# One attention and gated-MLP kernel: score operands moved 64 bytes, score products of 64 rows, down and output columns cut 256 and 320

## The chip, the cores and the metric

The kernel runs on one core of one Trainium2 chip. Five engines take part: TensorE (PE, matrix products; PEld is its loading of the stationary operand), VectorE (DVE), ScalarE (ACT), GpSimd (POOL), and SyncE (SP), whose queue issues most of the DMAs. The metric is the device time of one execution in microseconds (us); lower is better. Three executions of the kernel before took 2593.94, 2594.28 and 2596.97 us, so its median is 2594.28 us.

## What is computed

An attention block and a gated MLP read the same normalised input, and the MLP's result, through silu, gates the attention's:

```python
x = A_x                                      # 1 x 2048 x 576
xn = _layernorm(x, axis=-1)
s = _A_ref(xn, A_wqkv, A_wo)                 # 32 heads of 18: softmax(q k^T / sqrt(18)) v, then @ wo
g = _silu(_B_ref(xn, B_w_gate, B_w_up, B_w_down))   # ((xn @ w_gate) * (xn @ w_up)) @ w_down, 4608 wide
return x + s * g
```

Everything is float32. The kernel splits a float32 operand into a high part, which TensorE's float32r format holds, and a low part, the rest, and adds up high x high, high x low and low x high.

## The kernel before, in words

**Stages.** First the input is normalised, turned into columns (`xc`), and multiplied with `wqkv`: `qk_block` (L493) makes q and k, block by block of 128 columns, from a weight tile that is the stationary operand (`wgu`, `wq1` or `wq2`) and `xc` as the moving one; each block is 14 products of 128 rows by 512 columns, 13 with the weight tile and one with `ninth`. `v_block` (L556) makes v. Results go to DRAM. Then comes the long main stage, from about 193 to 2525 us, in which attention and MLP run side by side. Last, `L1469` multiplies the attention's columns with `wo` and the rows are finished.

**The main stage.** TensorE's array is used as two halves of 64 rows: rows 0 to 63 and rows 64 to 127, each with its own stream of products. Their kinds are:

- up and gate (`gu_op`, L813), 27 products of 512 columns to a group, up in half 0 and gate in half 1, with weights `wgu` stationary and `xc` moving;
- down (`down_op`, L874), `hs` stationary and `wd` moving. The 576 columns of the result go in two parts of `HALF` = 288, so a part is one product of 288 columns, 6 to a group in each half;
- score products for the row maxima (`a_item`, L709), one product of 512 columns each, 64 to a head, reduced by VectorE (L711). They stand in half 0, but for the first head, whose products go to both;
- score products for the exponentials (`b_item`, L761), 64 to a head as well, followed by ScalarE's exponential (L763). They stand in half 1, but for the end of the last head;
- value products (`pv_group`, L772), which use all 128 rows, so both halves stop for them.

**The score operands.** For each head a stack holds three times 18 rows of q or of k (high and low parts), `R` = 54 rows in each half of a tile. `turning` has one side and `whole0`/`whole1`, alternating by head, the other: `stacks_of` says which is which. L761 reads two rows more, 56: they carry minus the row maximum, high and low, against ones on the other side. L638 and L641 fill the three tiles with 1.0 on POOL, and `load_stack` (L322) brings the rows in by DMA on SP's queue.

**Where tiles lie.** The pools on the right-hand side of SBUF end at its top, so what a pool holds in all decides where it begins. In the program before, `turning`, `whole0` and `whole1` (pool `stk`) begin at bytes 204768, 212960 and 221152 of each partition, all 224 past a multiple of 256. `wq2`, in the pool `early` in the same place before it, lies 224 past a multiple of 256 as well. `xc`, `wgu`, `wq1`, `ninth`, `hs`, `wd` and `wos` all lie 160 past one. A column slice of 288 floats is 1152 bytes, so the second part of `wd` and of `wos` begins 32 past a multiple of 256. Every other slice that the products of 512 columns take begins a multiple of 512 bytes into its tile and keeps the tile's offset.

**The order.** The program is issued in an order that Python works out while it builds the kernel (`order`, L1326 on). Each half has a clock, `clk[0]` and `clk[1]`; the half whose clock is behind gets the next product: a score product if its bank is free and its due time has come, else down or up and gate. After a product the half's clock goes on by a planned duration: 0.231 us for 512 columns, 0.132 us for a part of down. `engine` keeps account of VectorE, ScalarE and POOL in the same way (0.685 us for a reduction, 0.596 for an exponential, 0.41 or 0.45 for the drain of a part of down). TensorE runs its instructions in the order of issue; nothing is decided on the chip.

**Drains.** A finished part of down is added to `acc` by VectorE (L937), or copied to `st` by ScalarE (L931) and added by POOL (L901).

Of the kernel before, what the change touches and what calls it, by code (L numbers as in the profile page):

```python
# [20 lines left out]
FT = mybir.dt.float32  # L21
FR = mybir.dt.float32r
I32 = mybir.dt.int32
AF = mybir.ActivationFunctionType
OP = mybir.AluOpType
# [16 lines left out]
def kernel(  # L42
# [10 lines left out]
    nc = tc.nc  # L53
    _, S, D = x.shape
    F = w_gate.shape[1]
    H = 32
    DH = D // H
    assert S == 2048 and D == 576 and F % 256 == 0
    NT = S // 128
    NCH = S // 512  # L60
    NF2 = F // 256
    HALF = D // 2
    scale = float(DH) ** -0.5
    PSUM = bass.MemoryType.PSUM

# [541 lines left out]
    for c in range(NCH):  # L607
        if c + 2 < NCH:
            load_x(c + 2)
        for b in range(3):  # L610
            qk_block(b, c)
            if c == 0 and b == 0:
                w_now(2)
        if c + 1 < NCH:
            to_columns(c + 1)
        for b in range(3, 6):
            qk_block(b, c)
            if c == 1 and b == 3:
                v_split(c)
            if b < 5 and c + 2 < NCH:  # L620
                norm(c + 2, (0, 1) if b == 3 else (2, 3))
            if c in (1, 2):
                x_store(c, range(3 * (b - 3), 3 * (b - 2)))
            if c == 0 and b == 3:
                v_fetch(1)
            if c == NCH - 1 and b == 3:
                w_now(3)
        if c == 1:
            w_fetch(3)
            for t in range(4):  # L630
                v_block(t)
            w_fetch(4)
        if c == 2:
            w_now(4)
    early.close()
    stk = ctx.enter_context(tc.tile_pool(name="stk", bufs=1, side="right", reuse_waits="tile"))
    turning = stk.tile([128, S], FR, name="turning")
    nc.gpsimd.memset(turning.bitcast(FT), 1.0)  # L638
    whole = [stk.tile([128, S], FR, name=f"whole{i}") for i in range(2)]
    for w in whole:  # L640
        nc.gpsimd.memset(w.bitcast(FT), 1.0)  # L641
    vmore = ExitStack()
    more_rows(vmore.enter_context(tc.tile_pool(name="vmore", bufs=1, side="right")), 2)
    g_load(0)
# [46 lines left out]
    with ExitStack() as mid:  # L691
# [3 lines left out]
        def load_v(g):  # L695
            vt[g] = mp.tile([128, NT, 2 * (DH + 1)], FT, name="vt", bufs=2)
            nc.sync.dma_start(vt[g].rearrange("p t (h d) -> p t h d", h=2), sv[:, 2 * g:2 * g + 2, :].rearrange("(t p) h d -> p t h d", p=128))

        mx = {}

        def a_item(h, i, r=0, tag="a"):

            t, c = divmod(i, 4)
            if i == 0:
                mx[h] = mp.tile([128, NT, 4], FT, name="mx", bufs=1)
            q, k = stacks_of(h, r)
            p = bank(tag, 2)
            rows = slice(64 * r, 64 * r + R)
            nc.tensor.matmul(p, q[rows, t * 128:(t + 1) * 128], k[rows, c * 512:(c + 1) * 512],  # L709
                             start=True, stop=True)  # L710
            nc.vector.tensor_reduce(mx[h][:, t, c:c + 1], p, axis=AX.X, op=OP.max)  # L711
# [42 lines left out]
        def b_item(h, i, r=1, tag="b"):  # L754
            t, c = divmod(i, 4)
            if c % 2 == 0:
                pt[t, c // 2] = mp.tile([128, 2, 512], FT, name="pt", bufs=PT)
            q, k = stacks_of(h, r)
            p = bank(tag, 2)
            rows = slice(64 * r, 64 * r + R + 2)  # L760
            nc.tensor.matmul(p, k[rows, t * 128:(t + 1) * 128], q[rows, c * 512:(c + 1) * 512],  # L761
                             start=True, stop=True)
            nc.scalar.activation(pt[t, c // 2][:, c % 2, :], p, AF.Exp, scale=scale)  # L763
# [37 lines left out]

        hs, us = {}, {}
        TERMS = [t for b in range(9) for t in ((b, b, 0), (9 + b, b, 0), (b, b, 1))]
        half = [slice(0, 64), slice(64, 128)]

        def gu_start(r, n):
            ready(gdone, n)
# [63 lines left out]
        def down_op(r, u, s, i, ps, n, by):  # L871
            own = alone(u, 2 * s + i)
            j, a, e = DTERMS[n]
            op = nc.tensor.matmul(ps[:, 0:HALF], hs[u][half[r], j, a, s * 128:(s + 1) * 128],  # L874
                             dw[u][half[r], j, e, i * HALF:(i + 1) * HALF],
                             start=(own or r == 0) and n == 0, stop=(own or r == 1) and n == len(DTERMS) - 1)
            if not own and r == 0 and n == len(DTERMS) - 1:
                handing[u, s, i] = by.nop()
                after(handing[u, s, i], op)
            if not own and r == 1 and n == 0:  # L880
                after(op, handing.pop((u, s, i)))
# [33 lines left out]

        def down_end(u, s, i, ps, act):
            c, q = units[u]
            cs = slice(i * HALF, (i + 1) * HALF)
            if q == 0 and c >= 2:
                ready(sdone, 4 * c - 8 + s)  # L920
            a = sums(4 * c + s)[:, cs]
            if s == 3:
                seen[u] = seen.get(u, 0) + 1
                if seen[u] == 2:
                    d_get(u + 1)
            if act:
                if q == 0:
                    nc.scalar.activation(a, ps[:, 0:HALF], AF.Copy)
                else:
                    st = mp.tile([128, HALF], FT, name="st", bufs=2)  # L930
                    nc.scalar.activation(st, ps[:, 0:HALF], AF.Copy)  # L931
                    sums_later.append((a, st, u, s))
                    return
            elif q == 0:
                nc.vector.tensor_copy(a, ps[:, 0:HALF])
            else:
                nc.vector.tensor_tensor(a, a, ps[:, 0:HALF], op=OP.add)  # L937
            down_summed(u, s)

        def down_summed(u, s):  # L940
# [80 lines left out]
            nc.sync.dma_start(wos[1].bitcast(FT), swo[:, 8:10, :])  # L1021

        passed, xdone, xhalf = {}, [], set()

        def stream(r, kind):

            def glu(n):
                c, q = units[n // 2]
                box = []
                for k in range(len(TERMS)):  # L1030
                    def work(k=k):
                        if k == 0:
                            box.append(gu_start(r, n))
                        gu_op(r, n, box[0], k)
                        if q == NF2 - 1 and n % 2 and k % 3 == 2 and c < NCH - 1:
                            b = k // 3
                            if (c, b) in xhalf:
                                x_block(c + 1, b)
                                there["x", c + 1, b] = moved(clk[r] + 0.5, 0.40)
                            xhalf.add((c, b))  # L1040
                        if n == 2 * len(units) - 1 and k == 13:
                            xdone.append(r)
                            if len(xdone) == 2:
                                wo_fetch()
                        if k == len(TERMS) - 1:
                            highs.append((gate_end if r else up_end)(n, box[0]))
                    end = (("DVE", 0.685) if r else ("ACT", 0.595)) if k == len(TERMS) - 1 else None
                    yield 0.231, k == 0, work, end, ("g", n, k), len(TERMS)

            def down(u, n):  # L1050
                own = alone(u, n)
# [2 lines left out]
                for k in range(len(DTERMS)):  # L1054
# [7 lines left out]
                    end = None  # L1062
                    if (own or r) and k == len(DTERMS) - 1:
                        end = (None, 0.0)
                    yield 0.132, (own or r == 0) and k == 0, work, end, ("d", u, 6 * n + k), len(DTERMS)

            if kind == "g":
                for n in range(2 * len(units)):
# [29 lines left out]
        due, jobs, rows_done = [], [], {}  # L1098
        there, queue = {}, [0.0]
        na = nb = 0  # L1100
        part_work = len(units) * (2 * 27 * 0.231 + 4 * 12 * 0.132)
        part = part_work + (TOTAL + N + LEAD) * 0.231
        span = part + H * NT * (0.858 + 0.06)
        QUICK, LAST = 0.65, 0.6
        pace = (PACE * span - QUICK * N - LAST * (N + LEAD)) / (TOTAL - N)
# [3 lines left out]
        def keep_course(now):  # L1109

            left = part_work - (gone[0] + gone[1]) / 2
            left += (2 * TOTAL - na - nb) * 0.1155 + (H * NT - nb // 4 + len(due)) * 0.918
            course[:] = [na, now, (EASE * left - TAIL - LAST * (N + LEAD)) / (TOTAL - na)]

        def a_goal(i):
# [24 lines left out]
        def a_next(r=0):  # L1140
# [5 lines left out]
            slot = turn[tag] % 2  # L1146
            turn[tag] += 1
            banks[tag][slot] = engine("DVE", clk[r] + 0.43, 0.685) + SPARE
            clk[r] += 0.231
            na += 1  # L1150
            if na % 32 == 0 and N <= na < TOTAL - N:
                keep_course(clk[r])
# [8 lines left out]
        def b_next(r=1):  # L1161
# [8 lines left out]
            turn[tag] += 1  # L1170
            end = engine("ACT", clk[r] + 0.43, 0.596)
            banks[tag][slot] = end + SPARE
            clk[r] += 0.231
            nb += 1
            if i % 4 == 3:
                due.append((h, i // 4, end + 0.1))
# [149 lines left out]
        def order():  # L1326
# [5 lines left out]
            while going(0) or going(1) or na < TOTAL or nb < TOTAL or due or jobs or soon or pool_later:  # L1332
# [33 lines left out]
                elif op is not None:  # L1366
# [14 lines left out]
                        kept[n, k // 6] = slots[0, kind]  # L1381
                    if end:
                        if kind == "d":
                            end = ("ACT", 0.41) if acts[-1] else ("DVE", 0.45)
                        if kind == "g" and r == 0 and n in by_dve:
                            end = ("DVE", 0.685)
                        done = engine(end[0], clk[r] + 0.20, end[1])
# [27 lines left out]
    with ExitStack() as end:  # L1415
# [45 lines left out]
        for i, t in enumerate(order):  # L1461
# [4 lines left out]
            for h in range(2):  # L1466
                for n, (a, e) in enumerate(PAIRS):
                    w = wos[0][:, a, :] if a < 8 else wos[1][:, a - 8, :]
                    nc.tensor.matmul(ps[h][:, 0:HALF], oc[:, e, :], w[:, h * HALF:(h + 1) * HALF],  # L1469
                                     start=n == 0, stop=n == len(PAIRS) - 1)  # L1470
            if i + 5 < NT:
                fetch_o(order[i + 5])
# [5 lines left out]
            g = gin.pop(t) if t < 12 else last_gates[t - 12]  # L1478
            xt = xi.pop(t)
            for h in range(2):  # L1480
                cs = slice(h * HALF, (h + 1) * HALF)
                nc.vector.tensor_tensor(y[:, cs], ps[h][:, 0:HALF], g[:, cs], op=OP.mult)
                if t == order[-1]:
                    nc.vector.tensor_tensor(y[:, cs], y[:, cs], xt[:, cs], op=OP.add)
                    nc.sync.dma_start(out2[t * 128:(t + 1) * 128, cs], y[:, cs])
# [34 lines left out]
```

## Time and profile before

| | |
|---|---|
| median of three runs | 2594.28 us |
| span of the profiled execution | 2590.2 us |
| TensorE, share of the span | 100% |
| VectorE, ScalarE, POOL | 70%, 60%, 26% |
| DMA, mean rate | 168 GB/s |
| first product of the main stage | 193.5 us |
| last down product begins | 2525.4 us |

The page gives for each engine its busy time and count of instructions; then the span in slices; then the chain of work that ended last, followed back from the end; then groups of instructions by line with the mean duration of one and the idle time before them. A product's recorded duration is modelled and overlaps the next one's, so the distance from start to start is what tells how fast TensorE goes. In the chain of waits and the timeline, each row has a start, a length, and how many instructions it merges (x94). `64*128 64x512` is a product of 64 rows by 128 stationary columns, with 512 moving columns.

### The profile page before, as it was taken

Reading aid. Unit: us, or ns where it says so; the run is one execution under the profiler, and the core shown is the slowest. Engines: PE = TensorE matmul, PEld = TensorE weight load, DVE = VectorE, ACT = ScalarE, POOL = GpSimd, SP = SyncE. Lnnn points to the kernel's source line nnn. Section 1 sums busy time; section 2 is a strip of 40 time slices with the busy share of each in tenths; the row PEclk is TensorE's granted clock in tenths of the full one; section 3 lists DMA queues with packets and bytes.
Section 4 is the critical chain, followed back from the end, with each engine's and each line's share of the span. In section 5 each row is a group of like instructions: output and inputs, shape, how many; then the busy total and the mean of one; then the engine's idle time right before and its main releaser. Section 6 shows DMA issues by size and latency. Waiting matters only on the chain.

```text
span 2590.2 us, 59629 instructions
## 1 busy us (share of the span) xinstructions
PE 2582.3 (100%) x24439; PEld 2124.4 (82%) x24439; DVE 1815.2 (70%) x2996; ACT 1551.5 (60%) x3092; POOL 677.0 (26%) x701
## 2 busy tenths in 40 slices
PE   9999999999999999999999999999999999999999
PEld 8899877888888888888877877778888877877889
DVE  7209777776777778777777877777777777777238
ACT  4224677766766666666666666666666666666621
POOL 3114444434431222222111222111111222221016
PEclk9999999999999999999999999999999999999999
DMA  7899767677653444444454443444444444443357
GB/s 237 258 301 260 200 184 196 184 189 214 178 189 111 141 164 136 150 162 160 143 166 148 142 142 126 137 146 159 121 158 124 145 150 142 133 139 112 125 202 253
DMA packets 186641, 435.65 MB, mean 168 GB/s; under 512 B 51104, under 2 KB 112192, under 8 KB 156160
## 3 DMA queue, kind: packets, MB, share of 16 engines
q1 hardware_dynamic: 184208, 423.88, 53.0%
q0 software_dynamic: 2160, 7.96, 0.8%
q8 instruction: 192, 3.15, 0.5%
q14 instruction: 81, 0.66, 0.1%
HBM read 315.16 MB, written 111.35 MB: 165 GB/s over the span
## 4 chain that ended last, share of the span: by engine, by line
PE 98%; DMA 1%; DVE 1%; SPq 0%; ACT 0%; issue 0%; DVEq 0%
PE pg L813 36%; PE pg L772 17%; PE pg L874 16%; PE pa L709 11%; PE pb L761 9%; PE pb L493 2%; PE pa L493 2%; PE pg L556 2%; PE pg L1469 1%; PE pb L1469 1%; PE pa L1469 1%; DMA oin<-sot 0%; PE pa L761 0%; DMA xin<-in_A_x_dram 0%; PE pg L402 0%; DVE mx L711 0%
## 5 line engine op out<-in xcount | busy, mean ns | idle before, releaser
L711 DVE TENSOR_REDUCE mx<-pa 128x1 f32<-128x512 f32 x2016 | 1349.2, 687 | 330.5 <-PE pa L709 151.5
L813 PE MATMUL pg<-xc,wgu 64*128 64x512 f32 x7776 | 1441.6, 391 | 0.0
L763 ACT ACTIVATE pt<-pb 128x512 f32<-128x512 f32 x2005 | 1145.0, 602 | 469.0 <-PE pb L761 347.3
L813 PEld LDWEIGHTS pg<-xc,wgu 64*128 64x128 f32 x7776 | 1074.9, 186 | 51.9 <-issue 1.0
L874 PE MATMUL pg<-wd,hs 64*128 64x288 f32 x6816 | 879.0, 293 | 0.0
L874 PEld LDWEIGHTS pg<-wd,hs 64*128 64x128 f32 x6816 | 816.3, 185 | 11.3 <-issue 0.8
L709 PE MATMUL pa<-whole,turning 54*128 54x512 f32 x1999 | 783.2, 399 | 0.3 <-DVE mx L711 0.3
L761 PE MATMUL pb<-whole,turning 56*128 56x512 f32 x1978 | 775.2, 398 | 0.0
L772 PE MATMUL pg<-pt,vt 128*32 128x512 f32 x4096 | 453.3, 594 | 0.1
L709 PEld LDWEIGHTS pa<-whole,turning 54*128 54x128 f32 x1999 | 363.3, 184 | 76.6 <-issue 53.0
L854 POOL TENSOR_TENSOR hs<-us,hs 128x512 fp32r<-128x512 f32 x144 | 186.1, 1292 | 865.8 <-ACT hs L838 612.4
L901 POOL TENSOR_TENSOR acc<-acc,st 128x288 f32<-128x288 f32 x284 | 229.5, 810 | 606.3 <-ACT st L931 314.4
L761 PEld LDWEIGHTS pb<-whole,turning 56*128 56x128 f32 x1978 | 360.1, 185 | 5.8
L772 PEld LDWEIGHTS pg<-pt,vt 128*32 128x32 f32 x4096 | 126.2, 110 | 285.1 <-issue 279.2
L778 DVE TENSOR_TENSOR oc<-oc,pg 128x512 f32<-128x512 f32 x35 | 24.1, 688 | 221.1 <-PE pg L772 207.0
L257 POOL TENSOR_TENSOR wgu<-wraw,wgu 128x384 fp32r<-128x384 f32 x108 | 108.2, 1015 | 212.8 <-ACT wgu L256 118.1
L776 ACT ACTIVATE oc<-pg 128x512 f32<-128x512 f32 x32 | 19.2, 599 | 229.4 <-PE pg L772 222.0
L937 DVE TENSOR_TENSOR acc<-acc,pg 128x288 f32<-128x288 f32 x261 | 116.3, 448 | 38.2 <-PE pg L874 35.4
L830 DVE TENSOR_TENSOR us<-pg,us 128x512 f32<-128x512 f32 x144 | 98.7, 685 | 54.9 <-PE pg L813 52.2
L931 ACT ACTIVATE st<-pg 128x288 f32<-128x288 f32 x284 | 117.1, 413 | 27.2 <-PE pg L874 20.0
L823 ACT ACTIVATE us<-pg 128x512 f32<-128x512 f32 x143 | 85.5, 598 | 76.2 <-PE pg L813 63.8
L838 ACT ACTIVATE hs<-us 128x512 fp32r<-128x512 f32 x142 | 89.4, 630 | 16.2 <-DVE us L830 15.8
(164 smaller groups left out, 1294.5 us busy)
## 6 DMA issues: line engine op xcount, KB each, us to landing
wgu<-swg SPq DMA_DIRECT2D x102, 1152.0 KB
wd<-swd SPq DMA_DIRECT2D x50, 1152.0 KB
swg<-wgu SPq DMA_DIRECT2D x36, 1152.0 KB
whole<-sqk SPq DMA_DIRECT2D x192, 144.0 KB
turning<-sqk SPq DMA_DIRECT2D x384, 72.0 KB
swd<-wd SPq DMA_DIRECT2D x18, 1152.0 KB
sqk<-hl SPq DMA_DIRECT2D x32, 512.0 KB
xc<-sx SPq DMA_DIRECT2D x24, 512.0 KB
```

The source lines that it names most:

```text
L257: nc.gpsimd.tensor_tensor(w[:, 9 + b:12 + b, :], raw[:, b:b + 3, :], w[:, b:b + 3, :].bitcast(FT), op=OP.subtract)
L709: nc.tensor.matmul(p, q[rows, t * 128:(t + 1) * 128], k[rows, c * 512:(c + 1) * 512], start=True, stop=True)
L711: nc.vector.tensor_reduce(mx[h][:, t, c:c + 1], p, axis=AX.X, op=OP.max)
L761: nc.tensor.matmul(p, k[rows, t * 128:(t + 1) * 128], q[rows, c * 512:(c + 1) * 512], start=True, stop=True)
L763: nc.scalar.activation(pt[t, c // 2][:, c % 2, :], p, AF.Exp, scale=scale)
L772: nc.tensor.matmul(p[32 * c:32 * c + 32, :], vt[h // 2][:, t, 6 * (h % 2):6 * (h % 2) + 32], pt[t, c // 2][:, c % 2, :], start=t == ts[0], ...
L813: nc.tensor.matmul(ps, gw[n][half[r], a, :], xg[i][half[r], e, :], start=k == 0, stop=k == len(TERMS) - 1)
L854: nc.gpsimd.tensor_tensor(hj[:, 1, :], h32, hj[:, 0, :].bitcast(FT), op=OP.subtract)
L874: op = nc.tensor.matmul(ps[:, 0:HALF], hs[u][half[r], j, a, s * 128:(s + 1) * 128], dw[u][half[r], j, e, i * HALF:(i + 1) * HALF], start=( ...
L901: nc.gpsimd.tensor_tensor(a, a, st, op=OP.add)
L931: nc.scalar.activation(st, ps[:, 0:HALF], AF.Copy)
L937: nc.vector.tensor_tensor(a, a, ps[:, 0:HALF], op=OP.add)
```

## The change

Four things are changed together.

1. A tile of 64 bytes, `gap`, is added to the pools `early` and `stk`. Both pools grow by 64 bytes at a fixed upper end, so `wq2` and the three score tiles begin 64 bytes lower: `turning` at 204704, which is 160 past a multiple of 256.
2. L709 and L761 read all 64 rows of a half instead of 54 and 56. So that the added rows add nothing, they are filled with 0 on one side and 1 on the other: rows 32 to 63 and 96 to 127 of each tile get a memset of their own, six in place of three; the loads bring in the rows below 54 as before.
3. The 576 columns of down and of the output product are cut 256 and 320 instead of 288 and 288, and so are the drains of those parts. The second part begins 1024 bytes into its row.
4. The planned durations in the order are changed: 512 columns 0.2267 us, parts of down 0.120 and 0.1467 us, and the drains of a part by its size.

```diff
+    PARTS = (slice(0, 256), slice(256, D))
+    WIDTH = (256, D - 256)
...
             if c == 0 and b == 0:
                 w_now(2)
+                ep.tile([128, 16], FT, name="gap")
...
     turning = stk.tile([128, S], FR, name="turning")
-    nc.gpsimd.memset(turning.bitcast(FT), 1.0)
     whole = [stk.tile([128, S], FR, name=f"whole{i}") for i in range(2)]
-    for w in whole:
-        nc.gpsimd.memset(w.bitcast(FT), 1.0)
+    stk.tile([128, 16], FT, name="gap")
+    for w, low, high in ((turning, 0.0, 1.0), (whole[0], 1.0, 0.0), (whole[1], 1.0, 0.0)):
+        nc.gpsimd.memset(w[32:64].bitcast(FT), low)
+        nc.gpsimd.memset(w[96:128].bitcast(FT), high)
...
+        half = [slice(0, 64), slice(64, 128)]
...
-            rows = slice(64 * r, 64 * r + R)
+            rows = half[r]
...
-            rows = slice(64 * r, 64 * r + R + 2)
+            rows = half[r]
...
-            op = nc.tensor.matmul(ps[:, 0:HALF], hs[u][half[r], j, a, s * 128:(s + 1) * 128],
-                             dw[u][half[r], j, e, i * HALF:(i + 1) * HALF],
+            op = nc.tensor.matmul(ps[:, 0:WIDTH[i]], hs[u][half[r], j, a, s * 128:(s + 1) * 128],
+                             dw[u][half[r], j, e, PARTS[i]],
...
-            cs = slice(i * HALF, (i + 1) * HALF)
+            cs, n = PARTS[i], WIDTH[i]
...
-                nc.vector.tensor_tensor(a, a, ps[:, 0:HALF], op=OP.add)
+                nc.vector.tensor_tensor(a, a, ps[:, 0:n], op=OP.add)
...
+        WIDE, SHORT = 0.2267, (0.120, 0.1467)
...
-                    yield 0.231, k == 0, work, end, ("g", n, k), len(TERMS)
+                    yield WIDE, k == 0, work, end, ("g", n, k), len(TERMS)
...
-                    yield 0.132, (own or r == 0) and k == 0, work, end, ("d", u, 6 * n + k), len(DTERMS)
+                    yield SHORT[i], (own or r == 0) and k == 0, work, end, ("d", u, 6 * n + k), len(DTERMS)
...
-        part_work = len(units) * (2 * 27 * 0.231 + 4 * 12 * 0.132)
-        part = part_work + (TOTAL + N + LEAD) * 0.231
+        part_work = len(units) * (2 * 27 * WIDE + 4 * 6 * sum(SHORT))
+        part = part_work + (TOTAL + N + LEAD) * WIDE
...
-            clk[r] += 0.231
+            clk[r] += WIDE
...
-                            end = ("ACT", 0.41) if acts[-1] else ("DVE", 0.45)
+                            end = ("ACT", (0.385, 0.44)[k // 6 % 2]) if acts[-1] else ("DVE", (0.42, 0.48)[k // 6 % 2])
...
-                    nc.tensor.matmul(ps[h][:, 0:HALF], oc[:, e, :], w[:, h * HALF:(h + 1) * HALF],
+                    nc.tensor.matmul(ps[h][:, 0:WIDTH[h]], oc[:, e, :], w[:, PARTS[h]],
...
-                nc.vector.tensor_tensor(y[:, cs], ps[h][:, 0:HALF], g[:, cs], op=OP.mult)
+                nc.vector.tensor_tensor(y[:, cs], ps[h][:, 0:WIDTH[h]], g[:, cs], op=OP.mult)
```

More of the change, by code (lines that the diff above doesn't have):

```diff
@@ L803 @@
         TERMS = [t for b in range(9) for t in ((b, b, 0), (9 + b, b, 0), (b, b, 1))]
-        half = [slice(0, 64), slice(64, 128)]
         def gu_start(r, n):
@@ L927, in down_end @@
                 if q == 0:
-                    nc.scalar.activation(a, ps[:, 0:HALF], AF.Copy)
+                    nc.scalar.activation(a, ps[:, 0:n], AF.Copy)
                 else:
-                    st = mp.tile([128, HALF], FT, name="st", bufs=2)
-                    nc.scalar.activation(st, ps[:, 0:HALF], AF.Copy)
+                    st = mp.tile([128, WIDTH[1]], FT, name="st", bufs=2)[:, 0:n]
+                    nc.scalar.activation(st, ps[:, 0:n], AF.Copy)
                     sums_later.append((a, st, u, s))
@@ L934, in down_end @@
             elif q == 0:
-                nc.vector.tensor_copy(a, ps[:, 0:HALF])
+                nc.vector.tensor_copy(a, ps[:, 0:n])
             else:
-                nc.vector.tensor_tensor(a, a, ps[:, 0:HALF], op=OP.add)
+                nc.vector.tensor_tensor(a, a, ps[:, 0:n], op=OP.add)
             down_summed(u, s)
@@ L1111, in keep_course @@
             left = part_work - (gone[0] + gone[1]) / 2
-            left += (2 * TOTAL - na - nb) * 0.1155 + (H * NT - nb // 4 + len(due)) * 0.918
+            left += (2 * TOTAL - na - nb) * WIDE / 2 + (H * NT - nb // 4 + len(due)) * 0.918
             course[:] = [na, now, (EASE * left - TAIL - LAST * (N + LEAD)) / (TOTAL - na)]
@@ L1172, in b_next @@
             banks[tag][slot] = end + SPARE
-            clk[r] += 0.231
+            clk[r] += WIDE
             nb += 1
@@ L1480 @@
             for h in range(2):
-                cs = slice(h * HALF, (h + 1) * HALF)
-                nc.vector.tensor_tensor(y[:, cs], ps[h][:, 0:HALF], g[:, cs], op=OP.mult)
+                cs = PARTS[h]
+                nc.vector.tensor_tensor(y[:, cs], ps[h][:, 0:WIDTH[h]], g[:, cs], op=OP.mult)
                 if t == order[-1]:
```

## The prediction

> **What bounds the kernel now.** I read the page from the top: busy shares, granted clock, the chain that ended last, then the groups.
>
> ```profile
> span 2590.2 us, 59629 instructions
> PE 2582.3 (100%) x24439; PEld 2124.4 (82%) x24439; DVE 1815.2 (70%) x2996; ACT 1551.5 (60%) x3092; POOL 677.0 (26%) x701
> PEclk9999999999999999999999999999999999999999
> PE 98%; DMA 1%; DVE 1%; SPq 0%; ACT 0%; issue 0%; DVEq 0%
> ```
>
> The chain is TensorE for 98% of the span at full clock; VectorE (70%) and ScalarE (60%) have slack. So the kernel is as long as its products, and the question is how far apart products start. Busy time doesn't tell: durations overlap and their ends are modelled. I take start-to-start distances instead.
>
> First the pace without score products. The chain of waits has a run of up and gate products (L813) near the end, and groups of the value product (L772) and the output product (L1469):
>
> ```profile
> 2452.87 10.64 PE pg L813 x94
> 2472.31 7.00 PE pg L772 x64
> 2480.97 11.22 PE pg L813 x98
> 2541.58 7.43 PE pg L1469 x56
> ```
>
> The L813 products stand in two streams, one for each array half, so 94 of them in 10.64 us are 47 per half: 226.4 ns for one 512-column product. The second run gives 11.22/49 = 229.0 ns. A 288-column product takes 7.43/56 = 132.7 ns; 64 value products take 7.00 us.
>
> Now the stage where score products (L709, L761) are mixed in. The table of stretches, asked for 200 to 2400 us line by line, in the order L813, L874, L709, L761, L772:
>
> ```profile
> 200.00:2400.00 2200.00, 1370.77 (x7282) 1015.09 (x7281) 1.00 0.51 157
> 200.00:2400.00 2200.00, 827.85 (x6336) 768.11 (x6336) 1.00 0.51 157
> 200.00:2400.00 2200.00, 794.94 (x2038) 369.55 (x2038) 1.00 0.51 157
> 200.00:2400.00 2200.00, 769.84 (x1966) 357.83 (x1966) 1.00 0.51 157
> 200.00:2400.00 2200.00, 432.12 (x3904) 120.25 (x3904) 1.00 0.51 157
> ```
>
> The first count in each row is products. 512-column ones: (7282+2038+1966)/2 = 5643 per half. At the undisturbed pace that is 5643 x 0.2264 = 1277.6 us; down 6336/2 x 0.1327 = 420.4; value products 61 x 7.00 = 427.0. Sum 2125.0 of 2200 us: **75 us are lost in this stage** to a slower pace and to waits. The timeline shows a slower pace that no wait explains:
>
> ```profile
> 1009.08 0.39 PE L709 MATMUL pa<-whole,turning 54*128 54x512 f32 x1
> ...
> 1009.31 0.40 PE L813 MATMUL pg<-xc,wgu 64*128 64x512 f32 x1
> ...
> 1009.55 0.39 PE L813 MATMUL pg<-xc,wgu 64*128 64x512 f32 x1
> ...
> 1009.78 0.39 PE L709 MATMUL pa<-whole,turning 54*128 54x512 f32 x1
> ...
> 1010.48 0.39 PE L709 MATMUL pa<-whole,turning 54*128 54x512 f32 x1
> ```
>
> At this time L709 runs in the first half, with two up products after each; the L874 and L761 rows left out between them are the other half's. From 1009.08 to 1010.48 are six products: 1.40/6 = **233.3 ns each, 6.9 above 226.4**. It isn't so everywhere: a row of six L813 in the same stage keeps the faster pace, of which the first and last are
>
> ```profile
> 1005.99 0.39 PE L813 MATMUL pg<-xc,wgu 64*128 64x512 f32 x1
> ...
> 1007.13 0.39 PE L813 MATMUL pg<-xc,wgu 64*128 64x512 f32 x1
> ```
>
> 1.14/5 = 228 ns, with no score product among them in their half. So the score products slow themselves and what stands next to them. The middle of 233.3 and 228 is 230.7 ns; I take it as the stage's mean (an estimate from two samples; the kernel plans with 0.231).
>
> **The change, part by part.**
>
> *Stacks and wq2 64 bytes lower.* What do the slow products have that the others lack? Other operands: turning and whole begin 224 bytes past a multiple of 256, while xc, wgu and hs are at 160. One more tile stands at 224, wq2, and that gives a test without score products. Timeline, two blocks of L493:
>
> ```profile
> 85.01 3.20 PE L493 MATMUL pa<-xc,wq 128*128 128x512 f32 x13
> 88.05 0.39 PE L493 MATMUL pa<-xc,ninth 128*128 128x512 f32 x1
> ...
> 97.91 3.11 PE L493 MATMUL pa<-xc,wgu 128*128 128x512 f32 x13
> 100.85 0.39 PE L493 MATMUL pa<-xc,ninth 128*128 128x512 f32 x1
> ```
>
> From the start of the first of 13 to the start of the ninth-block product after them: 3.04/13 = 233.8 ns with wq2 as stationary, 2.94/13 = 226.2 ns with wgu. Same line, rows, columns and moving tile; only the stationary tile differs. That is the 7 ns of the stage, found where nothing waits. So the offset between the two operands, or between one product and the next, sets the pace, and a stack at 160 should run like xc and wgu.
>
> Against it speaks the Trainium skill, page "TensorE: Matmul & The Clock Gate", section "Part 2: What happens when you issue a matmul": TensorE has two independent read ports, so loading the next stationary tile takes nothing from the running product. By that rule a tile's place makes no difference and this edit gives nothing. The two L493 blocks disagree (233.8 against 226.2 ns); I follow the blocks; the first rival has the rule's result.
>
> Price: 512-column products of the main stage, (7776+2048+2048)/2 = 5936 per half (L813 and the two score lines, 32 heads x 64 each). After the change I take 227.0 ns, between the two runs above and nearer 226.4, since 229.0 belongs to a run that restarts after a value group. Gain 5936 x (230.7 - 227.0) = **22.0 us**. Ends: if the mean is 233.3 and goes to 226.4, 41 us; if the stage already runs at 229.0, nothing. wq2: eight blocks of 13 products x 7.6 ns = 0.8 us.
>
> *64 rows to each score product.* Neither reads nor writes more columns, and the added rows are 0 against 1, so the product is the same. Nearest rows: weight loads of 54 rows and of 64 rows.
>
> ```profile
> L813 PEld LDWEIGHTS pg<-xc,wgu 64*128 64x128 f32 x7776 | 1074.9, 186 | 51.9 <-issue 1.0
> L709 PEld LDWEIGHTS pa<-whole,turning 54*128 54x128 f32 x1999 | 363.3, 184 | 76.6 <-issue 53.0
> ```
>
> 186 and 184 ns, beside 227 ns of product: I take 0. Ends: 2 ns x 2048 = 4 us lost if the load is on the path; up to the 22 us above if the row count, not the place, is what slows a score product. Both belong to one edit here, so the sum doesn't change.
>
> *256 and 320 columns.* From 288 (132.7) and 512 (226.4) a column costs 93.7/224 = 0.418 ns and a product 12.2 ns besides. So 256 takes 119.3 and 320 takes 146.1: 265.4 a pair, as 2 x 132.7. I take 0. Ends: the second part now starts 1152 bytes on (at 32 past a multiple of 256) and then 1024 (at 160); if it pays the stacks' 7 ns today, 1728 pairs per half x 7 = 12 us gained. If cost goes by steps of 128 columns, 320 costs as 384, 172.8 ns: 1728 x 26.7 = 46 us lost. The drains of a part go by columns as well:
>
> ```profile
> L937 DVE TENSOR_TENSOR acc<-acc,pg 128x288 f32<-128x288 f32 x261 | 116.3, 448 | 38.2 <-PE pg L874 35.4
> L931 ACT ACTIVATE st<-pg 128x288 f32<-128x288 f32 x284 | 117.1, 413 | 27.2 <-PE pg L874 20.0
> ```
>
> At one column per ns or less, 32 columns move some 30 ns from one part to the other, on engines with 30 to 40% slack: 0. After the last output product 32 more columns are multiplied and added, below 0.1 us.
>
> *Memsets.* Three full memsets become six of 32 rows. POOL's timeline, then the DMA queue's:
>
> ```profile
> 108.98 1.81 POOL L638 MEMSET turning<- 128x2048 f32 x1
> 110.83 3.56 POOL L641 MEMSET whole<- 128x2048 f32 x2
> 114.33 1.16 POOL L523 MEMSET vo<- 128x608 f32 x2
> 134.65 1.01 POOL L257 TENSOR_TENSOR wgu<-wraw,wgu 128x384 fp32r<-128x384 f32 x1 [19.15 <-ACT wgu L256]
> 122.32 1.09 SPq L322 DMA_DIRECT2D whole<-sqk  x3
> ```
>
> If a quarter costs what the whole did (most it can), they end at 108.98 + 6 x 1.81 = 119.8, vo's at 121.0. The first stack load is issued at 122.3 and POOL's next work is at 134.65, so both stay covered: 0. Were the cover gone by 5 us, TensorE has products of blocks 6 to 8 and of v until 193 before it needs a stack.
>
> *The ordering clocks.* They time no engine, but decide which product is issued when. If products really run at 226.7, 120 and 146.7, halves drift apart less between planned and real time and some of the 75 us of waits goes; if not, more comes. Waits are what the pace leaves: 75 - 5643 x 0.0043 = 51 us. I take 0 and ends of a quarter of it, 13 us either way.
>
> **Sum**, against the profiled execution: 2590.2 - 22.0 - 0.8 = 2567.4. The median of the runs is 2594.28, 4.1 above that span, so **2571.5 us**.
>
> **The rivals.**
>
> *The place is not the cause.* A score product would then be slow because it is a group of its own, with a wait before and a signal after it. Then L709 and its neighbours stay at 233 and only the order changes: 2594, within 0.2% of before (5 us, about what a measurement here can tell). For it: score products are the only single ones in the mix. Against it: the wq2 block, 13 products of one group. Chance 0.11. That the place gives nothing is also the result by the rule of the Trainium skill's page "TensorE: Matmul & The Clock Gate".
>
> *The products get faster and wait instead.* A score bank is freed by a reduction or an exponential:
>
> ```profile
> L711 DVE TENSOR_REDUCE mx<-pa 128x1 f32<-128x512 f32 x2016 | 1349.2, 687 | 330.5 <-PE pa L709 151.5
> ```
>
> If the new order meets banks that aren't free, half the gain goes back: 2571.5 + 11.4 = 2583. For it: every product moves in the order. Against it: VectorE waits 330 us in this line, mostly for TensorE, not the other way round. Chance 0.12.
>
> *Narrow products don't go by columns (slower).* Place: the 6912 down products; price 46 us by steps of 128, so 2571.5 + 46 = 2618. It decides once a pair costs over 265.4 + 22.8/1.728 = 278.6 ns. For it: no 256 or 320 is in this trace. Against it: 288 would then cost as 384 does, and 132.7 is far below 172.8. Chance, with any other loss that outweighs the gain, 0.07.
>
> **How the numbers follow.** The forecast (2557 to 2583, by the 41 and 0 us ends drawn in and the order's 13) has 0.70, and with the second case, faster by over 0.2% has 0.82; the first rival makes within 0.2% 0.11; slower 0.07. The range takes the forecast and the half-gain case, 2557 to 2589; left out are the unchanged and the slower case, 0.18.
>
> **What would show it.** Right: six products from L709 to the third L709 after it in 1.36 us instead of 1.40; blocks of 13 with wq in 2.94 us like wgu's; the six-row budget of 200 to 2400 us over the clean pace down from 75 to about 54. The 256 and 320 parts at 119 and 146 ns. Wrong: wq blocks at 2.94 while score neighbours stay at 233 (then it is not the place for the stacks); or the pace at 227 and the span unchanged (then waits took it); or pairs of down above 266 ns.

## The result, and the profile after

The changed kernel takes 2572.05 us (median of 4 runs, 2570.73 to 2573.03) against 2594.11 us before on the same chip: a ratio of 0.9915, 95% interval 0.9901 to 0.9929. The forecast was 2571.5 us. The page of the changed kernel, with its line numbers (L817 is up and gate, L714 and L766 are the score products, L716 the reduction):

```profile
span 2569.6 us, 59637 instructions
PE 2559.7 (100%) x24439; PEld 2112.7 (82%) x24439; DVE 1796.8 (70%) x2991; ACT 1552.2 (60%) x3097; POOL 689.0 (27%) x712
...
L716 DVE TENSOR_REDUCE mx<-pa 128x1 f32<-128x512 f32 x2016 | 1338.1, 686 | 348.7 <-PE pb L766 156.6
...
L714 PE MATMUL pa<-whole,turning 64*128 64x512 f32 x2000 | 776.0, 394 | 0.2
L766 PE MATMUL pb<-whole,turning 64*128 64x512 f32 x1986 | 772.6, 395 | 0.3 <-ACT pt L768 0.3
```

Before, the two score lines of the page were:

```profile
L709 PE MATMUL pa<-whole,turning 54*128 54x512 f32 x1999 | 783.2, 399 | 0.3 <-DVE mx L711 0.3
L761 PE MATMUL pb<-whole,turning 56*128 56x512 f32 x1978 | 775.2, 398 | 0.0
```

The same number of products, the same engine at 100%, VectorE still waiting for TensorE: only the span is 20.6 us shorter, and the recorded mean of a score product went from 399 and 398 to 394 and 395 ns. The table of stretches, 200 to 2400 us, line by line as before (up and gate, down, L714, L766, value products):

```profile
200.00:2400.00 2200.00, 1302.96 (x7408) 995.27 (x7404) 1.00 0.51 159
200.00:2400.00 2200.00, 786.57 (x6452) 729.69 (x6454) 1.00 0.51 159
200.00:2400.00 2200.00, 785.76 (x2033) 369.33 (x2033) 1.00 0.51 159
200.00:2400.00 2200.00, 762.30 (x1961) 356.72 (x1961) 1.00 0.51 159
200.00:2400.00 2200.00, 432.13 (x3904) 120.34 (x3904) 1.00 0.51 159
```

The same 2200 us now hold 126 more up and gate products and 116 more of down. By the sum of the prediction, (7408+2033+1961)/2 x 0.2264 + 6452/2 x 0.1327 + 61 x 7.00 = 2145.8 us of undisturbed work, so **54.2 us are lost where 75.0 were**. This number, "lost" below, is worked out in the same way for every kernel; it is the one to compare, since it doesn't depend on where in the span a product happens to stand.

In the timeline there are now stretches where score products run at the pace of a run without any:

```profile
1012.43 0.39 PE L714 MATMUL pa<-whole,turning 64*128 64x512 f32 x1
...
1012.88 0.39 PE L714 MATMUL pa<-whole,turning 64*128 64x512 f32 x1
...
1014.01 0.39 PE L714 MATMUL pa<-whole,turning 64*128 64x512 f32 x1
...
1014.47 0.39 PE L714 MATMUL pa<-whole,turning 64*128 64x512 f32 x1
...
1015.60 0.39 PE L714 MATMUL pa<-whole,turning 64*128 64x512 f32 x1
```

The distances are 0.45, 1.13, 0.46 and 1.13 us: two, five, two and five products of the half, 14 in 3.17 us, 226.4 ns each. And the block with wq2, together with a row of the output product:

```profile
85.31 3.11 PE L495 MATMUL pa<-xc,wq 128*128 128x512 f32 x13
88.26 0.39 PE L495 MATMUL pa<-xc,ninth 128*128 128x512 f32 x1
```

```profile
2520.66 7.47 PE pg L1474 x56
```

13 products with wq2 take 2.95 us instead of 3.04. The 56 output products of 256 and 320 columns take 7.47 us, where 56 of 288 took 7.43: 0.7 ns more for each.

Lastly the pace itself, from the start times of all products of a half (the order in which the kernel issues its products tells which half each is in): of the distances between one 512-column product and the next, I leave out those that hold a wait (over 14 ns above 226.7 ns, the pace of the fast stretches) and those over 10 ns below it. The mean of the rest went from 232.3 to 228.6 ns. A half has some 5,640 such distances in the main stage, so this is about 21 us. From its first product to its last down product that stage got 21.8 us shorter (193.5 to 2525.4 us before, 193.4 to 2503.5 after). The waits, all that a distance has over its pace where that is more than 14 ns, parts of down counted in, are 35 us a half before and after.

### The profile page after: what moved, and what is told of

It reads as the page before. It is cut to its first block, busy times and chain, and to the rows that moved or that the text cites. A ratio compares the mean times of both kernels' runs of the same rounds, so it can differ in the third digit from the quotient of the medians.

```text
span 2569.6 us, 59637 instructions
## 1 busy us (share of the span) xinstructions
PE 2559.7 (100%) x24439; PEld 2112.7 (82%) x24439; DVE 1796.8 (70%) x2991; ACT 1552.2 (60%) x3097; POOL 689.0 (27%) x712
## 4 chain that ended last, share of the span: by engine, by line
PE 98%; DVE 1%; DMA 0%; ACT 0%; SPq 0%; issue 0%; POOL 0%; DVEq 0%; ACTq 0%
PE pg L817 35%; PE pg L777 17%; PE pg L878 16%; PE pa L714 11%; PE pb L766 8%; PE pb L495 2%; PE pa L495 2%; PE pg L558 2%; PE pg L1474 1%; PE pb L1474 1%; PE pa L1474 1%; DVE mx L716 0%; DMA xin<-in_A_x_dram 0%; PE pa L766 0%; PE pg L404 0%; DMA oin<-sot 0%
## 5 line engine op out<-in xcount | busy, mean ns | idle before, releaser
L716 DVE TENSOR_REDUCE mx<-pa 128x1 f32<-128x512 f32 x2016 | 1338.1, 686 | 348.7 <-PE pb L766 156.6
L817 PE MATMUL pg<-xc,wgu 64*128 64x512 f32 x7776 | 1355.9, 388 | 0.0
L817 PEld LDWEIGHTS pg<-xc,wgu 64*128 64x128 f32 x7776 | 1041.2, 184 | 47.1
L878 PE MATMUL pg<-wd,hs 64*128 64x320 f32 (+1 forms) x6816 | 827.0, 294 | 0.2 <-ACT st L935 0.2
L878 PEld LDWEIGHTS pg<-wd,hs 64*128 64x128 f32 x6816 | 766.8, 185 | 13.0 <-issue 0.8
L714 PE MATMUL pa<-whole,turning 64*128 64x512 f32 x2000 | 776.0, 394 | 0.2
L766 PE MATMUL pb<-whole,turning 64*128 64x512 f32 x1986 | 772.6, 395 | 0.3 <-ACT pt L768 0.3
L714 PEld LDWEIGHTS pa<-whole,turning 64*128 64x128 f32 x2000 | 363.9, 184 | 68.4 <-issue 53.8
L766 PEld LDWEIGHTS pb<-whole,turning 64*128 64x128 f32 x1986 | 361.3, 184 | 5.8 <-ACT pt L768 1.1
L905 POOL TENSOR_TENSOR acc<-acc,st 128x256 f32<-128x256 f32 (+1 forms) x292 | 236.0, 813 | 472.3 <-ACT st L935 251.3
L935 ACT ACTIVATE st<-pg 128x256 f32<-128x256 f32 (+1 forms) x292 | 120.7, 413 | 28.4 <-PE pg L878 19.9
L941 DVE TENSOR_TENSOR acc<-acc,pg 128x256 f32<-128x256 f32 (+1 forms) x253 | 112.5, 446 | 28.7 <-PE pg L878 14.3
```

The lines of the kernel that those rows point to most:

```text
L817: nc.tensor.matmul(ps, gw[n][half[r], a, :], xg[i][half[r], e, :], start=k == 0, stop=k == len(TERMS) - 1)
L878: op = nc.tensor.matmul(ps[:, 0:WIDTH[i]], hs[u][half[r], j, a, s * 128:(s + 1) * 128], dw[u][half[r], j, e, PARTS[i]], start=(own or r == ...
L905: nc.gpsimd.tensor_tensor(a, a, st, op=OP.add)
L935: nc.scalar.activation(st, ps[:, 0:n], AF.Copy)
L941: nc.vector.tensor_tensor(a, a, ps[:, 0:n], op=OP.add)
```

## The experiments

The question was which of the four edits did it. The theory that I went in with was P, that the place of the operands sets the pace. Rival R was the row count, rival C the planned order, and later K, that the parts of 256 and 320 are needed too. All ratios are to the kernel before on the same chip.

| kernel | place | rows | parts | plan | us | ratio, 95% interval | lost, us |
|---|---|---|---|---|---|---|---|
| before | old | 54/56 | 288 | old | 2594.28 | | 75.0 |
| e1_place | new | 54/56 | 288 | old | 2593.11 | 0.9999 (0.9990 to 1.0008) | 76.4 |
| e2_rows | old | 64 | 288 | old | 2588.80 | 0.9981 (0.9972 to 0.9990) | 71.9 |
| e4_clocks | old | 54/56 | 288 | new | 2594.10 | 1.0004 (0.9995 to 1.0013) | 75.7 |
| e9_place_rows | new | 64 | 288 | old | 2575.00 | 0.9929 (0.9916 to 0.9941) | 58.6 |
| e3_after_no_place | old | 64 | 256/320 | new | 2589.60 | 0.9984 (0.9975 to 0.9992) | 70.1 |
| e6_after_no_rows | new | 54/56 | 256/320 | new | 2596.08 | 1.0010 (1.0001 to 1.0018) | 77.9 |
| e8_after_oldclocks | new | 64 | 256/320 | old | 2578.61 | 0.9944 (0.9932 to 0.9957) | 62.3 |
| e7_after_no_parts | new | 64 | 288 | new | 2568.80 | 0.9910 (0.9897 to 0.9924) | 52.6 |
| changed | new | 64 | 256/320 | new | 2572.05 | 0.9915 (0.9901 to 0.9929) | 54.2 |

**e1_place**, the two gaps alone:

```diff
                 w_now(2)
+                ep.tile([128, 16], FT, name="gap")
...
     whole = [stk.tile([128, S], FR, name=f"whole{i}") for i in range(2)]
+    stk.tile([128, 16], FT, name="gap")
```

> The kernel before with the two 64-byte gaps and nothing else: 54 and 56 rows, parts of 288, old planned durations. Theory P (the place of the operands sets the pace): almost the whole gain, 2574 us, 2568 to 2582; six products from one L709 to the third after it take 1.36 to 1.38 us, and 13 products with wq2 take 2.94 us. Rival R (the row count slows a score product): only the wq2 blocks get faster, 2593 us, 2588 to 2598, score neighbours at 233 ns. Rival C (the planned order gives the gain): 2594, 2588 to 2599.

Measured: no gain at all, though wq2's block is cured. Its timeline, the block with wq2 and the six products of the prediction, which the old plan issues in the same order:

```profile
84.69 3.11 PE L493 MATMUL pa<-xc,wq 128*128 128x512 f32 x13
87.64 0.39 PE L493 MATMUL pa<-xc,ninth 128*128 128x512 f32 x1
...
1009.10 0.40 PE L711 MATMUL pa<-whole,turning 54*128 54x512 f32 x1
...
1009.82 0.39 PE L711 MATMUL pa<-whole,turning 54*128 54x512 f32 x1
...
1010.51 0.39 PE L711 MATMUL pa<-whole,turning 54*128 54x512 f32 x1
```

13 products with wq2 in 2.95 us; the six score neighbours in 1.41 us, as slow as before (1.40). This is what the prediction had named as a sign of being wrong: wq blocks cured, score neighbours not. So the place is the whole story for wq2, whose products fill all 128 rows, and no part of it for a score product of 54 rows. P, as I had put it, has fallen.

**e2_rows**, 64 rows and the six memsets alone:

```diff
-            rows = slice(64 * r, 64 * r + R)
+            rows = slice(64 * r, 64 * r + 64)
...
-            rows = slice(64 * r, 64 * r + R + 2)
+            rows = slice(64 * r, 64 * r + 64)
...
```

> The kernel before with 64 rows to each score product and the six memsets, nothing else. Theory P: the pace stays, 2594 us, 2590 to 2600, score neighbours at 233 ns. Rival R: most of the gain, 2575 us, 2570 to 2583, score neighbours at 227 to 229 ns. Rival C: 2594.

Measured: 4.8 us faster, neither P's nothing nor R's 19. The rows alone aren't it either.

**e4_clocks**, the planned durations alone:

```diff
-                    yield 0.231, k == 0, work, end, ("g", n, k), len(TERMS)
+                    yield 0.2267, k == 0, work, end, ("g", n, k), len(TERMS)
...
-                    yield 0.132, (own or r == 0) and k == 0, work, end, ("d", u, 6 * n + k), len(DTERMS)
+                    yield 0.1333, (own or r == 0) and k == 0, work, end, ("d", u, 6 * n + k), len(DTERMS)
...
```

> The kernel before with the planned durations 0.2267 us for 512 columns and 0.1333 us for 288, nothing else. Theory P: products keep their pace, so the plan is now 1.9% too fast for them and the time is 2594 us or some us more, 2588 to 2606. Rival C: at least half the gain, 2572 to 2584. Rival R: as P.

Measured: no change. C alone is out.

**e3_after_no_place**, the changed kernel without the gaps:

```diff
-                ep.tile([128, 16], FT, name="gap")
...
-    stk.tile([128, 16], FT, name="gap")
```

> The changed kernel without its two gaps: stacks and wq2 at 224 past a multiple of 256 again; 64 rows, 256 and 320 columns and the new planned durations stay. Theory P: the gain is gone, 2593 us, 2587 to 2602, and 13 products with wq2 take 3.04 us. Rival R: 2573, 2569 to 2580. Rival C: 2573, 2569 to 2582.

Measured: 2589.60, so most of the gain goes with the place. That contradicts e1 unless the place needs another of the edits, of which the rows are the nearest. The sum of the two alone would be 0.5 + 4.8 = 5 us. The next four runs put this to the test.

**e9_place_rows**, both, with nothing else (the diffs of e1 and e2 together, order of issue as before):

> The kernel before with both gaps and 64 rows to each score product; parts of 288, old planned durations, so the order of issue is that of before. Theory B (the pace is right only when operands stand at one offset AND a product fills its 64 rows; either alone leaves the disturbance): 512-column products 1 to 3 ns over their shortest pace, 2577 us, 2570 to 2582. Rival S (the two effects only add, nothing and 4.8 us): 2588. Rival K (parts of 256 and 320 are needed too): 2584 to 2589.

Measured: 2575.00, 18 us faster where the sum of the parts is 5. Its table of stretches, up and gate (L815), down, L711, L763, value products:

```profile
200.00:2400.00 2200.00, 1363.82 (x7325) 999.47 (x7323) 1.00 0.51 158
200.00:2400.00 2200.00, 829.92 (x6381) 767.22 (x6381) 1.00 0.51 158
200.00:2400.00 2200.00, 789.29 (x2038) 368.53 (x2036) 1.00 0.51 158
200.00:2400.00 2200.00, 770.79 (x1984) 360.14 (x1984) 1.00 0.51 158
200.00:2400.00 2200.00, 438.19 (x3964) 122.26 (x3968) 1.00 0.51 158
```

(7325+2038+1984)/2 x 0.2264 + 6381/2 x 0.1327 + 3964/64 x 7.00 = 2141.4, so 58.6 lost. Mean distances as above, for up and gate and for score products: before 231.8 and 233.5 ns; place alone 232.1 and 233.3; rows alone 231.4 and 231.7; both 229.2 and 230.1. **Only both together bring the two halves near the 226.7 ns pace.** TensorE's order of issue is the same in all four.

**e6_after_no_rows**, the changed kernel with 54 and 56 rows:

```diff
-            rows = half[r]
+            rows = slice(64 * r, 64 * r + R)
...
-            rows = half[r]
+            rows = slice(64 * r, 64 * r + R + 2)
```

> The changed kernel with 54 and 56 rows to the score products again (the memsets stay). Theory B: the pace of before, 2593 us, 2588 to 2600. Rival S: 2572 + 4.8 = 2577.

Measured: 2596.08, and 77.9 lost. Without the rows everything is gone, as from the other side in e3.

**e7_after_no_parts**, the changed kernel with parts of 288:

```diff
-    PARTS = (slice(0, 256), slice(256, D))
-    WIDTH = (256, D - 256)
+    PARTS = (slice(0, HALF), slice(HALF, D))
+    WIDTH = (HALF, HALF)
...
-        WIDE, SHORT = 0.2267, (0.120, 0.1467)
+        WIDE, SHORT = 0.2267, (0.1333, 0.1333)
...
```

> The changed kernel with parts of 288 and 288 columns, planned at 0.1333 us each, drains planned as before; gaps, 64 rows and 0.2267 us stay. Theory B without the parts: same as changed, 2572 us, 2567 to 2578. Rival K: the second part at 32 past a multiple of 256 disturbs the pace as the stacks did, 2580 to 2589.

Measured: 2568.80; K is out. The parts of 256 and 320 save nothing. The medians say that they cost about 3 us (2572.05 against 2568.80 here, 2578.61 in e8 against 2575.00 in e9 with the old plan), but the intervals of each pair overlap, so that is no more than likely. By the output products a pair of parts costs 266.8 ns where two of 288 cost 265.4; over 1728 pairs a half that would be 2.4 us.

**e8_after_oldclocks**, the changed kernel with the old plan:

```diff
-        WIDE, SHORT = 0.2267, (0.120, 0.1467)
+        WIDE, SHORT = 0.231, (0.132, 0.132)
...
```

> The changed kernel with the old planned durations (0.231 us, 0.132 us for either part, drains 0.41 and 0.45): the operands as changed, the plan as before. Theory: the plan is worth little, 2575 us, 2570 to 2580. Rival (the plan matters once products keep 226.7 ns): 2582 or more, with the difference in waits over 14 ns and not in the pace.

Measured: 2578.61, within the theory's range but 6.6 us over the changed kernel; e9 against e7 gives 6.2. So the new plan is worth about 6 us once products keep the faster pace, and nothing before that (e4). It is worth them elsewhere than the rival said: from e9 to e7 the mean distance of all 512-column products goes from 229.5 to 228.6 ns, about 5 us, and the waits stay at 35 us a half. From e8 to the changed kernel, 5 us are in the pace as well, and some 3 in waits. Why an order changes the pace, these runs don't say.

Three runs then asked what disturbs, all from e7. TensorE's order of issue is that of e7 in each.

**e10_b_56_rows**, 56 rows for L766 alone, 64 for L714:

```diff
-            rows = half[r]
+            rows = slice(64 * r, 64 * r + R + 2)
             nc.tensor.matmul(p, k[rows, t * 128:(t + 1) * 128], q[rows, c * 512:(c + 1) * 512],
```

> The kernel of e7_after_no_parts, with 56 rows for the products of L761 alone; L709 keeps 64. Reading 1 (every short product disturbs itself and what is near it): half of the pace's gain gone, 2577 to 2585 us. Reading 2 (any short product disturbs the whole stage): 2588 to 2597, as e6. Reading 3 (only one kind matters): 2566 to 2572 if it is L709, as e6 if it is L761.

Measured: 2589.01 (ratio 0.9984, 0.9976 to 0.9993), 72.3 lost. One short kind in one half takes 20 of the 24 us: by the time that is reading 2, or nearly. The distances tell it otherwise. A stretch of e10 without waits, L714 in half 0 and L766 in half 1 (the rows left out are L817):

```profile
2294.88 0.39 PE L714 MATMUL pa<-whole,turning 64*128 64x512 f32 x1
2295.06 0.39 PE L766 MATMUL pb<-whole,turning 56*128 56x512 f32 x1
...
2295.33 0.39 PE L714 MATMUL pa<-whole,turning 64*128 64x512 f32 x1
2295.53 0.40 PE L766 MATMUL pb<-whole,turning 56*128 56x512 f32 x1
...
2296.47 0.39 PE L766 MATMUL pb<-whole,turning 56*128 56x512 f32 x1
2296.47 0.39 PE L714 MATMUL pa<-whole,turning 64*128 64x512 f32 x1
...
2296.92 0.39 PE L714 MATMUL pa<-whole,turning 64*128 64x512 f32 x1
2296.93 0.39 PE L766 MATMUL pb<-whole,turning 56*128 56x512 f32 x1
```

Half 0 has two, five and two products in 2.04 us, 226.7 ns each; at the same time half 1 has two, four and two in 1.87 us, 233.8 ns each. The whole stage is alike: the mean distance is 228.8 ns in half 0 (228.5 in e7) and 232.6 in half 1 (228.6 in e7). The short products slow their own half, as reading 1 had it, and half of the pace's gain is gone, 2.1 ns over both halves or 12 of the 20 us. Part of the rest is waits: half 0 waits 43 us, against 33 in e7, and half 1 38 in both. I read it as the faster half waiting for the slower one, since the plan counts both alike, and value products and the shared order of issue hold the halves together (in e10, e7 and before, no product starts more than about 0.7 us ahead of one issued before it); the run doesn't prove it.

**e11_stacks_128_off** and **e12_32_off**, other gaps:

```diff
-    stk.tile([128, 16], FT, name="gap")
+    stk.tile([128, 48], FT, name="gap")
```

```diff
-                ep.tile([128, 16], FT, name="gap")
+                ep.tile([128, 8], FT, name="gap")
...
-    stk.tile([128, 16], FT, name="gap")
+    stk.tile([128, 8], FT, name="gap")
```

> The kernel of e7_after_no_parts with the stacks 128 bytes lower still, at 32 past a multiple of 256 (the same place by 128, not by 256); wq2 stays at 160. If the offset counts by 128 bytes: the same, 2569 us, 2564 to 2575. If it counts by 256: the disturbance is back, 2584 to 2594, as e3.

> The kernel of e7_after_no_parts with gaps of 32 bytes: wq2 and the stacks at 192, 32 past the others. If any difference of offset disturbs: 13 products with wq2 in 3.00 to 3.04 us, and 2580 to 2594. If only half of 128 does: 2.94 us and 2569. If the delay is of the size of the difference: about 2.98 us for the 13 and about 2578 to 2584.

Measured: 2587.73 (0.9982, 0.9973 to 0.9991; 70.5 lost) and 2587.15 (0.9978, 0.9969 to 0.9987; 69.2 lost). With the stacks 128 bytes off, or 32, the gain shrinks to that of rows alone. In e12's timeline wq2 is slow again:

```profile
84.97 3.19 PE L495 MATMUL pa<-xc,wq 128*128 128x512 f32 x13
88.00 0.40 PE L495 MATMUL pa<-xc,ninth 128*128 128x512 f32 x1
```

3.03 us for 13 with 32 bytes off, 3.04 with 64, 2.95 with none. So a difference of 32, 64 or 128 bytes past a multiple of 256 disturbs, and by about the same. Both operands of a score product lie in the stacks and move together, so that they stand at one offset in every kernel here; what changes is their offset to the products before and after. The second part of `wd` stands 128 off as well in e7 and does no harm there; these runs don't say what makes it different.

**e13_plan_mean**, e7 planned with the distances that its own trace shows:

```diff
-        WIDE, SHORT = 0.2267, (0.1333, 0.1333)
+        WIDE, SHORT = 0.2286, (0.1325, 0.1325)
```

> The kernel of e7_after_no_parts, planned with the mean distances that its trace shows (0.2286 us for 512 columns, 0.1325 for 288) in place of the shortest ones. If a truer plan saves waits: 2563 to 2567. If the plan's exact value is worth nothing here: 2569, 2565 to 2574. From the old plan (0.231) against the new one, 6 us, a loss of 2 to 4 us is as likely.

Measured: 2566.33 (2565.74 to 2567.81 in 4 runs), ratio 0.9898, 0.9885 to 0.9912, and 52.3 lost. Every run of it is below every run of the changed kernel (from 2570.73), though the intervals of the two ratios still overlap by a little. It is the fastest version of this study: both gaps, 64 rows, parts of 288, and the measured mean in the plan. Against e7 its waits fell from 35 to 30 us a half, while the mean distance rose from 228.6 to 229.2 ns, a loss of over 3 us. How much of the 2.5 us to e7 is the plan's value and how much the luck of one order, one comparison doesn't tell.

## Why the prediction was right, and where it wasn't

- **The bound and the place of the gain: right.** TensorE's pace in the main stage was the limit. 75 us lost were to become about 54; 54.2 were measured. That it came out so closely, 2572.05 us against a forecast of 2571.5, is in part luck: place and rows gave 18 us where 22 were priced, and the plan, priced at 0, gave about 6.
- **The size of the pace: right in the difference, 1.6 ns low at both ends.** Forecast 230.7 to 227.0, measured over all distances without a wait 232.3 to 228.6: 3.7 ns both. But place and rows alone, in the old order (e9), reach 229.5 over all distances; the rest came with the new plan. The two samples of the prediction stood on the fast side, and the pace after is 226.4 in some stretches, not everywhere.
- **"A stack at 160 should run like xc and wgu": this step failed.** I carried the wq2 block over to the stacks, and passed over a thing in which they differ: wq2's products fill their rows. e1 shows that the place without the rows gives nothing: the wq2 block takes 2.95 us and six score neighbours still 1.41. That the row count might be the cause stood in the text, as an end of "I take 0"; that neither works without the other did not. The sum came out because the change made both edits, which I had counted as one term.
- **64 rows at 0: wrong in the same way.** Worth 4.8 us alone, and 18 us with the place (2593.11 to 2575.00).
- **wq2, 0.8 us: right** by its blocks, 3.04 to 2.95 us (8 x 0.09 = 0.7).
- **256 and 320 at 0: right**, if anything a cost of some us. The slower rival, cost by steps, is out: it would have shown in those 7.47 us.
- **Memsets at 0: right.** The main stage's first product stands at 193.4 us, before at 193.5.
- **The plan at 0 with ends of 13: the value was low, and the place wrong.** It is worth 6 us on the new operands. The prediction looked for it in the waits; from e9 to e7 these stay at 35 us a half, and the pace goes from 229.5 to 228.6 ns.
- **The rivals.** That the place is not the cause is half true: not alone. The reason that this rival gave, a group of its own with a wait before and a signal after, is out: in e9 the score products are as single as before, and their mean distance is 230.1 ns, not 233.5. The Trainium skill's page "TensorE: Matmul & The Clock Gate", section "Part 2: What happens when you issue a matmul", says that loading the next stationary tile takes nothing from the running product. The prediction took that to mean one time for wq2's block at all offsets; 2.95, 3.03 and 3.04 us say otherwise, though no run shows that it is the load that slows it. Faster products that wait instead didn't come: the waits stayed at 35 us a half.

So of the 22 us, place and rows together are 18 (e9), the plan about 6 on top (e9 to e7), and the parts take some 3 back.

What stays open is why. The runs show that operands at different offsets and products of fewer than 64 rows each slow the products of 512 columns, and that either is enough to lose most of the gain. What in TensorE or in the reads does it, no run here shows. Other row counts (60, say) and, with 512 columns, a moving tile at another offset with the stationary one in place weren't tried.

## What to carry to other kernels

Where TensorE is at 100% of the chain, measure the distance from start to start for one shape in several places of the trace; a shape that takes 226 ns in one run and 233 in another has something to give. Look then at where the tiles begin, past a multiple of 256 bytes, and at how many rows the products fill, and undo each edit by itself and together with the others: here each alone was worth nothing to 5 us and both 18. A plan made while building should use distances measured on the kernel as it now is; the old numbers cost 6 us on the new operands, and the new ones gained nothing on the old.

## What the runs showed of the hardware that was not expected

- A stationary tile that begins 32 or 64 bytes off the moving tile's place by 256 slows each 512-column product of 128 rows from 227 to 233 ns (13 in 2.95 us, or 3.03 and 3.04).
- With two streams in the halves, a score product of 54 or 56 rows among products of 64 does the same to its neighbours, and the right place doesn't help it: 1.41 us for six, against 1.40. It dies out in the up and gate products that follow in the half: the mean distance in the main stage of before is 233 ns after the score product, then 235, 232, 230 and 228.
- One slow stream costs both, but not in the same way: with 56 rows in half 1 alone (e10), half 1 goes to 232.6 ns, half 0 keeps 228.8 and waits 10 us more, and 72.3 - 52.6 = 20 us of loss are back.
